# Front outputs of a gated two-branch attention kernel summed in one PSUM bank, with a new order of the main loop

## The chip, the core and the metric

The kernel runs on one core of a Trainium2 chip. Its engines are TensorE (PE, matrix products, with its weight loads listed as PEld), VectorE (DVE), ScalarE (ACT), GpSimd (POOL) and SyncE (SP, which issues most DMAs). Matmul results go to PSUM, which has eight banks of 512 fp32 numbers per partition; SBUF holds everything else. The metric is the device time of one execution in microseconds.

## The reference

One sequence of 2048 tokens with 512 features goes through two attention branches, and a gate mixes them.

```python
g = sigmoid((x * gate_w).sum(-1, keepdims=True))
# A: 32 heads of 16; each token sees 8 tokens, at distances 0, 2, ..., 14
q, k, v = split(x @ wqkv)
a = softmax(q . k[window] * 16**-0.5) @ v[window] @ wo_A
# B: 32 query heads of 16, one shared key and value head, all 2048 x 2048 pairs
q = x @ wq;  k = x @ wk;  v = x @ wv
b = softmax(q @ k.T * 16**-0.5) @ v @ wo_B
out = g * a + (1 - g) * b
```

All is fp32. The weights wq and wk of branch B are drawn eight times larger than the others, so the softmax of branch B needs the maximum of each row of scores before the exponential.

## The kernel before, in words

The program is unrolled, and the order of its instructions is written out by a planner that runs while the kernel is built: it keeps a clock for PE, ACT and DVE (`clk`), advances them by estimated durations (`T_R` for a matmul, `T_RED2` and `T_RED1` for the reductions of a pair and of a single, `T_TTR` for a sum of half scores, and so on), notes in `free` when each PSUM bank can be written again, and in `tasks` what is due later. Each engine then carries out its own list in that order and waits on semaphores where data or a buffer is not ready.

Branch B is cut into 32 units (a block of 512 queries, four heads) and each unit into 16 steps (128 keys), 512 steps in all. The work has three parts.

**Maxima.** For each unit, scores are computed once only to find row maxima: 64 half maxima of 128 queries x 512 keys each, 2048 in all. `fill_pair` computes two of them (heads on the even and on the odd 64 partitions, two matmuls side by side in the array) into the two-bank tile `pm` (`m2`), and DVE reduces both (L331). `fill_one` does one, into `ps` (`m1`) or, in the front, `po` (L342). In the front there is a cheaper form for two key blocks at a time: `fill_diff` computes half the difference (L390 into pm), ACT takes its absolute value (L399, `dd`), and `fill_sum` computes half the sum into ps and po, where DVE adds and takes the maximum in one instruction (L409). That form needs the half keys, which `half_keys` makes with the projections (L369). The maxima of a unit are collected in a small tile `mx`, which is first set to a very negative number by ACT (L305, the first nine). When a unit is complete, they are transposed, split and stored into two spare rows of its query tile `qst` (`shift_a` to `shift_d`).

**The front.** After a start of some 29 us, `stream` works through 14 query projections (`lumps` "q", 512 columns) and 64 projections for branch A, v and the gate ("a", 384 or 402 columns). Each output sums 12 products of 128 rows (x and the weights are split into two parts for precision). Each product is cut into its upper and lower 64 rows, which run side by side in the array as two lanes (`b` = 0, 1); the upper rows sum in the first and the lower in the second bank of an `eb` tile (pe), outputs alternate between the two tiles, and the very last uses pm. Both lanes advance by one product per turn of the loop. Maxima are put in between: a single takes the place of one lane's product, a pair or a diff goes between two. When an output is done, ACT copies both banks (`queries_post`: L201; `a_post`: L240 and L241, for v and the gate L243 and L244), and POOL adds the halves (L204, L250, L252, L253). The query is then split again (L210, L211) and stored; SP stores two finished A projections at a time from a `stage` tile, of which there are two. POOL meanwhile computes branch A itself (L518 to L578) from what was stored. At most eight units are stacked (`NB`) in the front, so that at most 512 half maxima can be made there.

**The main loop.** Each step has: the scores and exponential of the first two heads (`exp_pair(s, 0)`, L448 on PE and L450 on ACT, bank tile `e0`), one pair of maxima, the scores and exponential of the second two heads (`exp_pair(s, 1)`, `e1`), one single of maxima, and the weighted sums of the step before (`weighted`, L458, into po). The order is that of the tuple `order`; singles are left out where pairs alone suffice (`singles`) or where the bank is not free within `M1S` of the planner's clock. Three times four output rows are projected in a phase of their own (`out_phase`, through `stream`), with maxima in between; a phase starts when the maxima's lead falls below `LEAD` units or at a fixed step. The last four rows are spread over the last steps, when no maxima are left.

## Time and profile before

| | us |
|---|---|
| median of 3 runs | 1525.32 (1525.28 to 1527.5) |
| span of the profiled execution, first to last instruction | 1523.8 |
| PE busy | 1489.5 |
| ACT busy | 1243.8 |
| DVE busy | 1235.3 |
| POOL busy | 1030.6 |
| first and last projection matmul of the front start | 29.4 and 278.0 |
| first and last weighted sum of the main loop start | 279.5 and 1510.8 |

The profiled execution has its span of 1523.8 us and no time of its own beside it; the runs are 1.5 us longer in the median, which takes in what lies before the first and after the last instruction. The granted TensorE clock is 0.997 over the run.

How the rows read: in a group, "L399 ACT ACTIVATE dd<-pm ... x166 | 92.2, 610 | 21.8" means that line 399 wrote tile dd from tile pm on ACT 166 times, was busy for 92.2 us, took 610 ns each, and that ACT was idle for 21.8 us before them. In a stretch ("106.80:276.80") each engine's busy time is followed by its number of instructions; then come the granted clock, the DMA share and GB/s. In a timeline row the start and duration come first, merged instructions are counted (x2), and a bracket tells the idle time before and what ended it. In a wait row ("PEld pm L390 <- ACT dd L399: 13.6, 39, 1.6") the numbers are total us, times, and the longest. Matmul durations overlap: the spacing of starts is what PE needs.

### The profile page before, as it was taken

How to read it: one execution, taken by the hardware profiler on the slowest of the kernel's cores; microseconds unless marked ns; L12 is line 12 of the kernel's file. 1: busy time of each engine (PE TensorE's matmuls, PEld its weight loads, DVE VectorE, ACT ScalarE, POOL GpSimd, SP SyncE). 2: the span in 40 equal slices, each digit the busy share in tenths (PEclk: the TensorE clock that was granted, in tenths of full speed). 3: DMA queues.
4: the chain of work that ended last, by engine and by line, in shares of the span. 5: the costliest groups of instructions: out<-in, count | busy, mean ns of one | idle time of the engine just before them, and what ended most of it. 6: DMA issues, size and time to landing. Idle time of an engine off the chain costs nothing.

```text
span 1523.8 us, 28901 instructions
## 1 busy us (share of the span) xinstructions
PE 1489.5 (98%) x10920; PEld 706.1 (46%) x10920; DVE 1235.3 (81%) x1755; ACT 1243.8 (82%) x1590; POOL 1030.6 (68%) x1769
## 2 busy tenths in 40 slices
PE   7999999999999999999999999999999999999988
PEld 4989888533333333333333453333345335433333
DVE  5976666788888888889888998898899889888701
ACT  4558987889999899999999759999975995799774
POOL 7866988787888888888888888889887004100020
PEclk9999999999999999999999999999999999999999
DMA  6744223121121121120220112202201000000000
GB/s 216 202 119 131 90 75 126 33 75 47 50 76 47 41 75 44 43 76 22 66 77 14 65 33 68 68 12 69 69 19 33 1 1 16 15 2 2 1 1 28
DMA packets 43908, 85.63 MB, mean 56 GB/s; under 512 B 9520, under 2 KB 25960, under 8 KB 39672
## 3 DMA queue, kind: packets, MB, share of 16 engines
q1 hardware_dynamic: 36200, 44.00, 9.8%
q0 software_dynamic: 6560, 37.95, 7.5%
q8 instruction: 86, 1.41, 0.4%
q10 hardware_dynamic: 1008, 1.84, 0.3%
q14 instruction: 54, 0.44, 0.1%
HBM read 57.97 MB, written 25.25 MB: 55 GB/s over the span
## 4 chain that ended last, share of the span: by engine, by line
PE 89%; ACT 4%; DVE 4%; POOL 1%; issue 1%; DMA 1%; DVEq 0%; ACTq 0%; POOLq 0%
PE po L458 32%; PE pe L448 22%; PE pm L311 9%; PE ps L311 8%; PE pe L1004 8%; PE pe L709 4%; DVE mx L331 2%; ACT dd L399 2%; ACT pexp L450 1%; PE pm L766 1%; PE pm L390 1%; PE pe L174 1%; DVE mx L342 1%; PE po L390 0%; PE ps L390 0%
## 5 line engine op out<-in xcount | busy, mean ns | idle before, releaser
L450 ACT ACTIVATE pexp<-pe 128x1024 f32<-128x1024 f32 x1024 | 992.9, 1022 | 116.3 <-PE pe L448 116.0
L331 DVE TENSOR_REDUCE mx<-pm 128x2 f32<-128x1024 f32 x554 | 676.6, 1221 | 125.7 <-PE pm L311 120.4
L458 PE MATMUL po<-pexp,vst 128*32 128x512 f32 x4096 | 547.1, 606 | 0.6 <-DVE tt L472 0.5
L448 PE MATMUL pe<-qst,kst 64*128 64x512 f32 x2048 | 460.9, 448 | 6.8 <-ACT pexp L450 2.6
L448 PEld LDWEIGHTS pe<-qst,kst 64*128 64x128 f32 x2048 | 190.6, 184 | 506.7 <-ACT pexp L450 488.4
L342 DVE TENSOR_REDUCE mx<-ps 128x1 f32<-128x512 f32 x565 | 384.4, 680 | 5.7 <-PE ps L311 5.0
L311 PE MATMUL pm<-kst,qst 62*128 62x512 f32 x1122 | 235.7, 407 | 3.1 <-DVE mx L331 2.4
L311 PE MATMUL ps<-kst,qst 62*128 62x512 f32 x565 | 228.6, 405 | 0.7 <-DVE mx L342 0.7
L518 POOL TENSOR_TENSOR pr<-aext 128x256 f32<-128x256 f32 x256 | 182.0, 736 | 0.2
L578 POOL TENSOR_TENSOR oa<-oa,av 128x256 f32<-128x256 f32 x224 | 163.9, 732 | 15.4
L458 PEld LDWEIGHTS po<-pexp,vst 128*32 128x32 f32 x4096 | 80.7, 108 | 182.5 <-issue 170.7
L575 POOL TENSOR_TENSOR av<-aext,lg 128x256 f32<-128x256 f32 x224 | 139.3, 622 | 12.8
L484 POOL TENSOR_TENSOR rl<-rl,gate_t 128x16 f32<-128x16 f32 x31 | 6.8, 220 | 182.6 <-DVE rl L478 182.4
L311 PEld LDWEIGHTS pm<-kst,qst 62*128 62x128 f32 x1122 | 108.9, 186 | 24.7 <-DVE mx L331 21.3
L311 PEld LDWEIGHTS ps<-kst,qst 62*128 62x128 f32 x565 | 105.3, 186 | 22.4 <-DVE mx L342 18.4
L399 ACT ACTIVATE dd<-pm 128x512 f32<-128x512 f32 x166 | 92.2, 610 | 21.8 <-DVE mx L409 10.8
L1004 PE MATMUL pe<-wah,xh 64*128 64x384 f32 (+1 forms) x504 | 108.5, 338 | 0.0
L1004 PE MATMUL pe<-wal,xh 64*128 64x384 f32 (+1 forms) x504 | 108.5, 337 | 0.0
L1004 PE MATMUL pe<-wah,xl 64*128 64x384 f32 (+1 forms) x504 | 108.4, 337 | 0.0
L409 DVE CUSTOM_DVE_ANT_0 dd<-ps,dd 128x512 f32<-128x512 f32 x83 | 57.4, 692 | 58.8 <-PE ps L390 29.4
L524 POOL TENSOR_TENSOR tr<-pr 128x512 f32<-128x512 f32 x64 | 81.7, 1276 | 4.2
L250 POOL TENSOR_TENSOR stage<-stage,two 128x384 f32<-128x384 f32 x64 | 65.0, 1015 | 26.3 <-ACT two L241 13.4
(185 smaller groups left out, 1596.7 us busy)
## 6 DMA issues: line engine op xcount, KB each, us to landing
aext<-ad POOLq DMA_DIRECT2D x32, 1056.0 KB, 5.4
ad<-stage SPq DMA_DIRECT2D x32, 384.0 KB
qst<-qd SPq DMA_DIRECT2D x64, 128.0 KB
xraw<-xt SPq DMA_DIRECT2D x16, 256.0 KB
qd<-qhi SPq DMA_DIRECT2D x16, 256.0 KB
qd<-qlo SPq DMA_DIRECT2D x16, 256.0 KB
qst<-qd SPq DMA_DIRECT2D x64, 64.0 KB
qst<-ml SPq DMA_DIRECT2D x228, 2.0 KB
```

What stands on the lines that cost most here:

```text
L311: nc.tensor.matmul(dst, qst[v % NB][b:b + 62, pr, t * P:(t + 1) * P], kst[b:b + 62, kc * 512:(kc + 1) * 512], start=True, stop=True)
L331: nc.vector.tensor_reduce(m[:, :, pr, t, kc], dst, AX.X, ALU.max)
L342: nc.vector.tensor_reduce(m[:, odd, pr, t, kc:kc + 1], dst, AX.X, ALU.max)
L399: nc.scalar.activation(dd[0][:, odd], m2[:, odd, :], AF.Abs)
L448: nc.tensor.matmul(bank[:, odd, :], kst[b:b + 64, kt * P:(kt + 1) * P], qst[u % NB][b:b + 64, pr, :], start=True, stop=True)
L450: nc.scalar.activation(e, bank, AF.Exp, scale=SCALE)
L458: nc.tensor.matmul(po[32 * i:32 * i + 32, :], vst[:, kt, :], pexp[s, i // 2][:, i % 2, :], start=(kt == 0), stop=(kt == NJ - 1))
L518: nc.gpsimd.tensor_mul(pr[:, k], q, e[:, o:o + NH, AC:2 * AC])
L524: nc.gpsimd.tensor_add(nx, cur[:, :, 0:n], cur[:, :, n:2 * n])
L575: nc.gpsimd.tensor_mul(av, e[:, o:o + NH, 2 * AC:].rearrange("p j (h d) -> p j h d", d=DH), lg[:, w].unsqueeze(3).to_broadcast([P, NH, AG, ...
L578: nc.gpsimd.tensor_add(ao, ao, av)
L1004: nc.tensor.matmul(front[2 if x == last else x % 2][0][:, b, :n], l[h], r[h], start=(i == 0), stop=(i == 3 * C - 1))
```

## The change

1. In the front, both row halves of an output are summed in the same bank. Four single banks (`fb`, the halves of the two eb tiles) are used in turn, and the last two outputs use po and ps. The two lanes never write the same bank at once: the lower lane starts an output only when the upper lane has finished it and when a maximum (or an exponential) that was issued behind the upper lane's last product has been read, by the planner's clock (`marks`, `behind`); the first lower matmul is also given a dependency on that reading instruction. ACT copies an output once, and POOL's adds are gone. A query output is copied twice from PSUM, once as it is and once rounded, in place of the copy, the add and the split.
2. `front_stream` takes the place of `stream` in the front: it holds banks back for the half keys (`wanted`) instead of waiting for them, uses a lane only where the planner allows it (`below`, `after_upper`), and lets a diff wait until ACT's clock is at most `ACTS` ahead.
3. The first values of `mx` are set by ACT for two units alone and by POOL for the others, when the unit two before is complete.
4. In the main loop the single goes between the pair and the second scores: `(0, "m2", "m1", 1)` in place of `(0, "m2", 1, "m1")`.
5. Planner times: `T_R` 0.235, `T_TTR` 0.74, a projection product 0.1755 or 0.2335.

```diff
-LEAD, M2S, M1S = 1.5, 0.5, 0.3
-T_R, T_LAT, T_EXP, T_RED2, T_RED1, T_W, T_TTR = 0.23, 0.20, 0.92, 1.14, 0.61, 1.21, 0.66
+ACTS, LEAD, M2S, M1S = 0.5, 1.5, 0.5, 0.3
+T_R, T_LAT, T_EXP, T_RED2, T_RED1, T_W, T_TTR = 0.235, 0.20, 0.92, 1.14, 0.61, 1.21, 0.74
...
-    def queries_post(m, bank):
+    def queries_post(m, bank, key):
-        two = p0.tile([P, 2, 512], F32, name="two", tag="wqr", bufs=1)
-        nc.scalar.activation(two, bank, AF.Copy)
-        at = after("act", clk["pe"] + T_LAT, 0.92)
         own = p0.tile([P, 512], F32, name="qraw", bufs=1)
-        nc.gpsimd.tensor_add(own, two[:, 0], two[:, 1])
-        pool = max(pool, 1e3 * at) + 1400
         hi, lo = parts_of()
+        nc.scalar.activation(own, bank, AF.Copy)
+        nc.scalar.activation(hi, bank, AF.Copy)
+        at = after("act", clk["pe"] + T_LAT, 1.1)
+        free[key] = at + 0.1
...
-            nc.scalar.activation(hi, own, AF.Copy)
             nc.gpsimd.tensor_sub(lo, own, hi.bitcast(F32))
-            pool = max(pool, 1e3 * after("act", 0, 0.6)) + 1400
+            pool = max(pool, 1e3 * at) + 1400
...
-    def a_post(gg, j, x):
-        nonlocal pool
-        (bank, key), n = front[x], GN + (0 if gg else VN)
-        settle("add", 1)
+    def a_post(gg, j, bank, key):
         if j % 2 == 0:
             settle("store", 1)
             stage["t"] = p1.tile([P, GC, 2, AN], F32, name="stage", bufs=2)
         st = stage["t"]
-        if gg == 0 and j < 3:
-            two = wp.tile([P, GN + VN], F32, name="two", tag="aext", bufs=2)
-        else:
-            two = (p2 if j % 3 else pm)[0].tile([P, GN + VN], F32, name="two", tag=("two", "raw", "own")[j % 3], bufs=1)
-        own = st[:, :, j % 2, :]
-        nc.scalar.activation(own, bank[:, 0, :GN].rearrange("p (g n) -> p g n", g=GC), AF.Copy)
-        nc.scalar.activation(two[:, :n], bank[:, 1, :n], AF.Copy)
+        nc.scalar.activation(st[:, :, j % 2, :], bank[:, :GN].rearrange("p (g n) -> p g n", g=GC), AF.Copy)
         if gg == 0:
-            nc.scalar.activation(vst[:, j, 0:DH], bank[:, 0, GN:GN + DH], AF.Copy)
-            nc.scalar.activation(gate[:, 1, j:j + 1], bank[:, 0, GN + DH:GN + DH + 1], AF.Copy)
-        at = after("act", clk["pe"] + T_LAT, 0.8 if gg else 1.2)
+            nc.scalar.activation(vst[:, j, 0:DH], bank[:, GN:GN + DH], AF.Copy)
+            nc.scalar.activation(gate[:, 1, j:j + 1], bank[:, GN + DH:GN + DH + 1], AF.Copy)
+        at = after("act", clk["pe"] + T_LAT, 0.42 if gg else 0.8)
         free[key] = at + 0.1
-        def rest():
-            nonlocal pool
-            nc.gpsimd.tensor_add(own, own, two[:, :GN].rearrange("p (g n) -> p g n", g=GC))
-            if gg == 0:
-                nc.gpsimd.tensor_add(vst[:, j, 0:DH], vst[:, j, 0:DH], two[:, GN:GN + DH])
-                nc.gpsimd.tensor_add(gate[:, 1, j:j + 1], gate[:, 1, j:j + 1], two[:, GN + DH:GN + DH + 1])
-            pool = max(pool, 1e3 * at) + (1000 if gg else 1450)
-            if j % 2 == 1:
-                dst = ad[gg * GC:(gg + 1) * GC, HALO:, :].rearrange("g (p j) n -> p g (j n)", j=NJ)
-                tasks.append((pool / 1e3 + 0.5, lambda: nc.sync.dma_start(dst[:, :, (j - 1) * AN:(j + 1) * AN], st.rearrange("p g j n -> p g (j n)")), (), "store"))
-            if j == NJ - 1:
-                tasks.append((pool / 1e3 + 1.0, whole, (gg,)))
-        tasks.append((at, rest, (), "add"))
+        if j % 2 == 1:
+            dst = ad[gg * GC:(gg + 1) * GC, HALO:, :].rearrange("g (p j) n -> p g (j n)", j=NJ)
+            tasks.append((at + 0.3, lambda: nc.sync.dma_start(dst[:, :, (j - 1) * AN:(j + 1) * AN], st.rearrange("p g j n -> p g (j n)")), (), "store"))
+        if j == NJ - 1:
+            tasks.append((at + 1.0, whole, (gg,)))
...
+    marks, ups = [], [0]
+    def mark(inst, end):
+        marks.append((ups[0], end, inst.ins.name))
...
     def unit_tile(v):
         if v not in mx:
             mx[v] = wp.tile([P, 2, 2, 4, 4], F32, name="mx", bufs=3)
-            if v <= NB:
+            if v < 2:
                 nc.scalar.activation(mx[v].rearrange("p b i t k -> p (b i t k)"), ident[:, 0:64], AF.Identity, scale=0.0, bias=mk[:, 6:7])
+            elif v <= NB:
+                nc.gpsimd.memset(mx[v], -FMAX)
             left[v] = NF // NU
         return mx[v]
...
+            if v + 2 < NU:
+                unit_tile(v + 2)
...
+        got = nc.vector.tensor_reduce(m[:, :, pr, t, kc], dst, AX.X, ALU.max)
         free[key] = after("dve", after("pe", 0, T_R) + T_LAT, T_RED2) + 0.08
+        mark(got, free[key])
...
-    def half_keys(g):
-        keys = ("m2", "m2") if g == 0 else ("m1", "po")
+    wanted = []
+    def half_keys(g, keys):
         clk["pe"] = max(clk["pe"], *(free[k] for k in keys))
...
+            got = nc.scalar.activation(dd[0][:, odd], m2[:, odd, :], AF.Abs)
             ready_d[odd] = after("act", at, 0.52) + 0.1
+            mark(got, ready_d[odd])
...
+    fb = [eb[1][:, 0, :], eb[1][:, 1, :], eb[0][:, 0, :], eb[0][:, 1, :]]
+    def home(x):
+        if x >= last - 1:
+            return ((po, "po"), (m1, "m1"))[x - last + 1]
+        return fb[x % 4], f"f{x % 4}"
+    def begin(x):
+        lump = lumps[x]
+        if lump == ("a", 0, 3):
+            half_sel()
+        elif lump in (("a", 0, 4), ("a", 0, 6)):
+            wanted.append((1, ("m1", "po")) if lump[2] == 4 else (0, ("m2", "m2")))
+        items[x] = queries(lump[1]) if lump[0] == "q" else a_project(*lump[1:])
+    def begin_exp(k):
+        free[f"e{k}"] = max(free.get(f"f{y}", 0.0) for y in (2 - 2 * k, 3 - 2 * k))
+        exp_pair(0, k)
     def mm(b, at):
-        nonlocal pool
         x, i = at
         lump = lumps[x]
         if x not in items:
-            if lump[0] == "a" and lump[1:] == (0, 0):
-                settle("rest", 0)
-                p0.release()
-                branch_a()
-                pm.append(tc.alloc_tile_pool(name="maxima", bufs=1, side="right"))
-            if lump == ("a", 0, 3):
-                half_sel()
-            elif lump in (("a", 0, 4), ("a", 0, 6)):
-                half_keys(1 if lump[2] == 4 else 0)
-            items[x] = queries(lump[1]) if lump[0] == "q" else a_project(*lump[1:])
-            clk["pe"] = max(clk["pe"], free["m2" if x == last else f"e{x % 2}"])
+            begin(x)
         n = 512 if lump[0] == "q" else GN + (0 if lump[1] else VN)
         l, r = items[x][i]
         h = slice(64 * b, 64 * b + 64)
-        nc.tensor.matmul(front[2 if x == last else x % 2][0][:, b, :n], l[h], r[h], start=(i == 0), stop=(i == 3 * C - 1))
-        return T_R if n == 512 else 0.18
+        inst = nc.tensor.matmul(home(x)[0][:, :n], l[h], r[h], start=(i == 0 and b == 0), stop=(i == 3 * C - 1 and b == 1))
+        dur = 0.2335 if n == 512 else 0.1755
+        if b == 0 and x == last - 2 and i == 3 * C - 4:
+            ended.add(1)
+        if b == 0 and i == 3 * C - 1:
+            ups[0] = x + 1
+            if x == last:
+                begin_exp(1)
+        if b == 1 and i == 0:
+            tc.add_manual_dep(inst.ins, behind(x), mybir.DependencyInfo(mybir.DependencyClass.Sync, mybir.DependencyReason.DATA))
+        return dur
...
-        if x == last - 1 and i == 3 * C - 2:
-            ended.add(1)
-        if x == last and i in (2, 7):
-            exp_pair(0, int(i == 2))
+        if lump == ("a", 0, 0) and i == 1:
+            settle("rest", 0)
+            p0.release()
+            branch_a()
+            pm.append(tc.alloc_tile_pool(name="maxima", bufs=1, side="right"))
+        if x == last and i == 9:
+            begin_exp(0)
         if i < 3 * C - 1:
             return
+        items.pop(x)
+        bank, key = home(x)
         if lump[0] == "q":
             m = lump[1]
-            queries_post(m, eb[x % 2])
-            free[f"e{x % 2}"] = clk["act"]
+            queries_post(m, bank, key)
             ahead_wa(0, m - 4)
         else:
             gg, j = lump[1:]
-            a_post(gg, j, 2 if x == last else x % 2)
+            a_post(gg, j, bank, key)
             if gg + 1 < C:
                 ahead_wa(gg + 1, j - 2)
...
-    front = [(eb[0], "e0"), (eb[1], "e1"), (m2, "m2")]
-    stream([(x, i) for x in range(len(lumps)) for i in range(3 * C)], mm, done_mm, True)
+    def fits(key, slack=0.1):
+        return free[key] <= clk["pe"] + slack and not (wanted and key in wanted[0][1])
+    def front_stream(seq):
+        at, told = [0, 0], 0
+        may = (below, after_upper)
+        while told < len(seq):
+            if wanted and all(free[k] <= clk["pe"] + 0.1 for k in wanted[0][1]) and not pend:
+                half_keys(*wanted.pop(0))
+            single, odd = None, -1
+            if pend:
+                k = pend[0][4]
+                if free[("m1", "po")[k]] <= clk["pe"] + 0.1 and ready_d[k] <= clk["pe"] + 0.4:
+                    single, odd = fill_sum, k
+            elif ended or paired() and not half:
+                pass
+            elif half or slots and fillable():
+                for dst, key in ((m1, "m1"), (po, "po")):
+                    if single is None and fits(key):
+                        single, odd = lambda dst=dst, key=key: fill_one(dst, key), half[0][4] if half else 0
+            dur = 0.0
+            for b in (0, 1) if odd != 1 else (1, 0):
+                if b == odd:
+                    now = clk["pe"]
+                    single()
+                    clk["pe"] = now
+                elif at[b] < len(seq) and may[b](*seq[at[b]]):
+                    dur = max(dur, mm(b, seq[at[b]]))
+                    at[b] += 1
+            after("pe", 0, dur or T_R)
+            if ended:
+                if slots and fillable() and fits("m2"):
+                    fill_pair(m2, "m2")
+            elif paired():
+                if not half and not pend and not wanted and max(free["m2"], clk["dve"] - 1.2, clk["act"] - ACTS) <= clk["pe"] + 0.1:
+                    fill_diff()
+            elif slots and fillable() and fits("m2"):
+                fill_pair(m2, "m2")
+            while told < at[1]:
+                told += 1
+                done_mm(seq[told - 1])
+    def behind(x):
+        marks[:] = [m for m in marks if m[0] > x]
+        return next((m[2] for m in marks if m[1] + 0.1 <= clk["pe"]), None)
+    def after_upper(x, i):
+        return i > 0 or behind(x) is not None
+    def below(x, i):
+        return i > 0 or free.get(home(x)[1], 0.0) <= clk["pe"] + 0.1 and (lumps[x] != ("a", 0, 3) or bool(pm)) and not (pend and x >= last - 1)
+    front_stream([(x, i) for x in range(len(lumps)) for i in range(3 * C)])
...
-        order = (0, "m2", 1, "m1") if s > 1 else (1, "m2", 0, "m1") if s else ()
+        order = (0, "m2", "m1", 1) if s > 1 else (1, "m2", "m1", 0) if s else ()
```

36 lines of the change are left out of this document (12 added, 24 removed).

## The prediction

> **What bounds the kernel now.** I read the page first, then the busy time by stretches, then one step of the main loop in the timeline, then the waits.
>
> ```profile
> span 1523.8 us, 28901 instructions
> PE 1489.5 (98%) x10920; PEld 706.1 (46%) x10920; DVE 1235.3 (81%) x1755; ACT 1243.8 (82%) x1590; POOL 1030.6 (68%) x1769
> PE 89%; ACT 4%; DVE 4%; POOL 1%; issue 1%; DMA 1%; DVEq 0%; ACTq 0%; POOLq 0%
> ...
> 106.80:276.80 170.00, 166.47 (x1659) 149.88 (x1658) 112.79 (x349) 143.07 (x336) 135.23 (x220) 1.00 0.33 102
> 279.45:850.00 570.55, 567.15 (x3935) 203.36 (x3935) 502.72 (x629) 519.66 (x571) 484.39 (x909) 1.00 0.16 53
> 1309.00:1432.00 123.00, 122.99 (x862) 43.84 (x854) 108.64 (x130) 111.44 (x118) 8.82 (x20) 1.00 0.01 1
> 1441.00:1510.00 69.00, 62.71 (x357) 25.11 (x357) 2.16 (x5) 49.55 (x60) 12.64 (x16) 0.98 0.00 1
> ```
>
> The columns of a stretch are PE, PEld, DVE, ACT and POOL. TensorE is busy nearly throughout, and the chain is 89% PE. Two stages matter: the front's diff stage (106.8 to 276.8 us) and the main loop (279 to about 1441 us with maxima, then to 1510 without). In the main loop PE is full and ACT and DVE are both within some 10% of it, so I looked at which wait is closest behind PE. That takes one step:
>
> ```profile
> 599.55 1.94 ACT L450 ACTIVATE pexp<-pe 128x1024 f32<-128x1024 f32 x2 [0.19 <-PE pe L448]
> ...
> 601.08 0.19 PEld L448 LDWEIGHTS pe<-qst,kst 64*128 64x128 f32 x2 [0.84 <-ACT pexp L450]
> 601.09 0.49 PE L448 MATMUL pe<-qst,kst 64*128 64x512 f32 x2
> ...
> 601.42 0.40 PE L311 MATMUL pm<-kst,qst 62*128 62x512 f32 x2
> 601.54 0.19 PEld L448 LDWEIGHTS pe<-qst,kst 64*128 64x128 f32 x2 [0.16 <-ACT pexp L450]
> ...
> 601.66 0.39 PE L448 MATMUL pe<-qst,kst 64*128 64x512 f32 x2
> ...
> 601.86 1.23 DVE L331 TENSOR_REDUCE mx<-pm 128x2 f32<-128x1024 f32 x1 [0.32 <-PE pm L311]
> 601.89 0.40 PE L311 MATMUL ps<-kst,qst 62*128 62x512 f32 x1
> ...
> 603.00 0.68 DVE L342 TENSOR_REDUCE mx<-ps 128x1 f32<-128x512 f32 x1
> ...
> 603.55 0.40 PE L311 MATMUL pm<-kst,qst 62*128 62x512 f32 x2
> ```
>
> A step is 603.55 - 601.42 = 2.13 us. On PE the pair (pm) is followed 0.24 us later by the second scores (pe) and again 0.23 us later by the single (ps). The second scores' weight load comes 0.05 us after ACT ends (599.55 + 1.94 = 601.49, load at 601.54). The single had no wait: its bank is free at 603.00 + 0.68 = 603.68 and it is next wanted at 603.55 + 0.24 + 0.23 = 604.02. So in this order the ACT release only just suffices and the DVE release has about 0.3 us to spare.
>
> **The change part by part.**
>
> **Second evictions.**
>
> ```profile
> L399 ACT ACTIVATE dd<-pm 128x512 f32<-128x512 f32 x166 | 92.2, 610 | 21.8 <-DVE mx L409 10.8 <-PE pm L390 10.6
> L241 ACT ACTIVATE two<-pe 128x384 f32<-128x384 f32 (+1 forms) x63 | 31.5, 499 | 0.0
> L201 ACT ACTIVATE two<-pe 128x1024 f32<-128x1024 f32 x14 | 14.4, 1027 | 5.7 <-PE pe L1004 5.1
> L210 ACT ACTIVATE qhi<-qraw 128x512 fp32r<-128x512 f32 x14 | 8.9, 632 | 21.2 <-POOL qraw L204 14.1 <-DMA qd<-qhi 7.1
> L250 POOL TENSOR_TENSOR stage<-stage,two 128x384 f32<-128x384 f32 x64 | 65.0, 1015 | 26.3 <-ACT two L241 13.4
> PEld pm L390 <- ACT dd L399: 13.6, 39, 1.6
> PE ps L369 <- issue: 1.7, 1, 1.7
> ```
>
> ACT loses 31.5 us of copies for the projections. A query output keeps two copies out of PSUM at about 0.61 us (the L399 row has that form), 17.1 us in place of 14.4 + 8.9, so 6 us less. ACT in the front falls by some 37 us. PE does not get this as such, since ACT was not full (143.07 of 170). What PE can get back is at most the 13.6 us in which a diff's weight load waited for ACT; matmuls already under way cover about half, so I take -6 (0 to -10). POOL loses 65.0 us and the smaller adds of the queries, v and gate. POOL is almost idle late in the main loop (8.82 of 123), so that is worth 0. Each store of a projection no longer waits for POOL and is issued on SP's queue some 1 us earlier, ahead of the small transfers of the maxima that stood before it; 0 as well, hidden behind the two stage tiles, and where they ran out ACT would stand until a store has landed, with the Abs copies queued behind it. The wait of the half keys for two banks at once becomes a condition, which gives back the 1.7 us of the L369 row.
>
> **One bank, lower rows behind.** The trace of before has no held-back row half. Its cost is a delay that is paid once: the lower lane starts after the upper lane's 12 matmuls and after one maximum that was issued behind them has been read. The wait for that maximum is new; behind the waiting matmul everything on PE is queued, ACT and DVE with it.
>
> ```profile
> 179.73 0.50 PE L390 MATMUL pm<-kcd,qst 62*128 62x512 f32 x2
> 180.07 0.34 PE L1004 MATMUL pe<-wah,xh 64*128 64x384 f32 x2
> 180.24 0.34 PE L1004 MATMUL pe<-wal,xh 64*128 64x384 f32 x2
> ```
>
> Pairs of projection matmuls follow each other by 0.175 us, so 12 are 2.1 us; the maximum's way adds about 0.4 + 1.23 (the pm matmul until DVE starts, the reduction). I take +4; the ends are +2 (the early scores fill the idle lane at the end) and +8 (lag grows to a second output). Later lower halves find their maximum long read, 0 while the planner's order holds. The Trainium skill (PSUM — Partial Sum Buffer, section "PSUM bank collisions raise a hardware error") says that different row tiles cannot write one bank at the same time and that software has to keep them apart. No row of before shows it; were it not so here, the hold could be dropped, this term would be 0 and the sum 4 us lower.
>
> **More rounds of diffs.** A round (two diff matmuls, two sums, four half maxima) costs PE 0.34 + 0.235 = 0.575 us, from 179.73 to 180.07 and the single spacing in the step above.
>
> ```profile
> L409 DVE CUSTOM_DVE_ANT_0 dd<-ps,dd 128x512 f32<-128x512 f32 x83 | 57.4, 692 | 58.8 <-PE ps L390 29.4
> 106.80:276.80 170.00, 151.71 (x1328) 138.98 (x1327) 1.00 0.33 102
> ```
>
> Before, 83 rounds stand in 170 us, one in 2.05, among 1328/2 = 664 pairs (the second row is L1004 alone). Two Abs copies (2 x 0.61) and two sums on DVE (2 x 0.69 and a read-out each) allow one in about 1.8 once ACT has half the copies. I take 93 rounds: +10 x 0.575 = +6 us, and 40 half maxima more. The ends are 75 rounds (the new conditions on ACT and on wanted banks hold them back) and 100, since eight stacked units hold 512 half maxima and the front has 52 singles + 2 x 28 pairs + 4 x 83 = 440 now (the rows of L331 and of L342, the third of L342 in the main loop):
>
> ```profile
> 29.40:106.80 77.40, 34.25 (x28) 1.00 0.58 160
> 29.40:106.80 77.40, 33.47 (x52) 1.00 0.58 160
> 279.45:1441.00 1161.55, 375.95 (x553) 1.00 0.13 41
> ```
>
> The front: -6 - 1.7 + 4 + 6 = +2.3, range -10 to +12.
>
> **First values by GpSimd.** Most of the small ACT writes that set them go to POOL, and a unit's is issued two units early; 0, with POOL's idle 35 of 170 us as cover. Without that cover a round's sum on DVE would wait for POOL's queue, a few us a unit.
>
> **Single between pair and second scores.** PE's own work per step is the same. The single now wants its bank right after the pair: at 603.55 + 0.24 = 603.79. It is free at 603.68, its load can start 0.05 later, and a matmul behind a load that was waited for starts 0.10 later (0.49 against 0.39 in the rows at 601.09 and 601.66): 603.83 to 603.84. It is some 0.05 us late, and the second scores and the weighted sums queue behind it, since PE takes them in order. After a late step DVE gains that 0.05, so every other step is late: 0.025 us a step. DVE sets it, by 0.44 us from pair to reduction, 1.14 to the second one, and 0.68. The main loop has 553 singles, some 45 of them in its three output phases and a few in pauses; I take 485 steps with both: +12 us. Ends: 0, and +0.05 in each, +24. The Trainium skill (PSUM — Partial Sum Buffer, section "Engine vs sequencer instructions") says that matmuls start and complete in program order though a weight load may be pulled ahead. By that rule the late single delays all behind it and the sum is as here; by its opposite, scores that pass a waiting single, this term would be 0 and the time 1520. The step above shows the issued order, so the trace agrees as far as it goes.
>
> ACT's release of the second bank gets 0.24 us of slack. Eight copies of 0.63 us per run overrun ACT's 0.19 us idle in a step, which this hides: -2.
>
> ```profile
> L75 ACT ACTIVATE woh<-os 128x512 fp32r<-128x512 f32 x8 | 5.1, 632 | 0.0
> ```
>
> **Fewer singles.** Forty half maxima made in the front leave forty steps without a single. Such a step is bound by ACT's 1.94 us plus about 0.05 in place of 2.155: -6 (0 to -10). The new planner times change only the order, 0.
>
> **The sum.** 1523.8 + 2.3 + 12 - 2 - 6 = 1530.1 us of span. The runs shown have a median of 1525.3, 1.5 over this span, which I take for what lies around it: 1532.
>
> **The rivals.**
> The single's wait does not bind (faster). If DVE reads the pair 0.05 us earlier, or the planner's skipped singles give DVE air often enough, the term of 12 is 0 and the rest is 1523.8 + 2.3 - 2 - 6 + 1.5 = 1520; with the front's low end 1507. For it: the overrun is only 0.05 us, the size of one semaphore. Against: DVE's chain is the same to 0.01 us in each step I looked at. It decides at a time from pair to free bank of 2.21 us, against 603.68 - 601.42 = 2.26.
>
> The held-back lower half starves the front (slower). Late marks or blocked banks leave half of PE empty again and again: 64 projections x 0.25 to 0.35 us = 16 to 22 us instead of 4, which gives 1544 to 1550. For it: a mark needs a maximum, and in the queries' stage DVE is full. Against: four banks, and a lag once built stays.
>
> The copies taken from ACT do nothing (no gain in the front): the front is PE's 664 x 0.175 = 116 and 83 x 0.575 = 48, so 164 of 170 us are matmuls already, and the 6 us do not come: 1538. This lies within the forecast's own range.
>
> **How the numbers follow.** Forecast 0.50 with its own range 1525 to 1541, first rival 0.32, second 0.18. A measurement of this kernel can tell about 0.2%, 3 us, from no change. Faster takes most of the first rival and a little of the forecast, 0.32; same 0.10; slower 0.58. 1510 to 1549 leaves out the far end of the first and of the second.
>
> **What would show it.** Of the main loop: steps of 2.13 and 2.18 us in turn, the load of ps waiting about 0.05 us for L342, the 0.16 us waits of pe gone. Of the front: it ends near 281 us with about 93 rounds, no copy of a second half, the first lower half some 4 us behind. Wrong would be: main steps still at 2.13 us, or a front that ends more than 10 us earlier or later.

## The result and the profile after

The changed kernel takes 1629.01 us (median of 4 runs, 1624.84 to 1631.02), the kernel before beside it 1526.34 us. The ratio is 1.0666, 95% interval 1.0648 to 1.0683: some 102 us slower, far outside the forecast's range.

The page of the changed kernel:

```profile
span 1623.0 us, 28701 instructions
PE 1523.4 (94%) x10920; PEld 713.2 (44%) x10920; DVE 1233.0 (76%) x1736; ACT 1219.8 (75%) x1531; POOL 948.6 (58%) x1670
PE 81%; ACT 7%; DVE 4%; issue 1%; DMA 0%; POOL 0%; SPq 0%; DVEq 0%; ACTq 0%
```

TensorE was busy for 98% of the span and is now for 94%, and the chain of work that ended last has 7% ACT in place of 4%. Where that lies is told by the stretches (columns PE, PEld, DVE, ACT, POOL, clock). The first fence is the front before. The second is of after: the whole front, its part with diffs, and the first 478 us of the main loop.

```profile
29.60:278.00 248.40, 241.51 (x2320) 217.46 (x2318) 182.41 (x442) 183.42 (x411) 197.09 (x290) 1.00 0.41 120
```

```profile
32.00:371.10 339.10, 272.68 (x2359) 231.54 (x2360) 202.61 (x476) 159.22 (x354) 152.75 (x263) 0.99 0.31 94
106.80:371.10 264.30, 205.69 (x1847) 178.66 (x1847) 140.81 (x394) 140.25 (x315) 122.42 (x232) 0.99 0.25 80
372.40:850.00 477.60, 471.63 (x3248) 165.84 (x3247) 398.20 (x490) 431.68 (x472) 403.00 (x757) 0.99 0.17 54
```

The front grew from 248.4 to 339.1 us, with only 39 matmuls more. TensorE stands for 66 of those 339 us, and no other engine is full: ACT and POOL do less than before. From the first to the last weight load of the weighted sums the main loop went from 1230.8 (279.5 to 1510.3) to 1237.4 us (372.4 to 1609.8). So 90.7 of the 99.2 us of span are the front's. What TensorE waited for there, in total us, times, and the longest (PE rows and PEld rows tell of the same time and are not added):

```profile
PE pe L992 <- ACT stage L230: 44.4, 44, 1.9
PE pe L992 <- ACT gate L233: 13.7, 15, 1.8
PE pe L992 <- ACT qhi L203: 7.6, 11, 1.3
PE pe L992 <- DVE kst L179: 1.9, 1, 1.9
PEld pe L992 <- ACT stage L230: 57.9, 43, 2.3
ACT dd L390 <- PE pm L381: 101.5, 87, 2.6
```

Projection products wait 70 times for ACT's copies of finished outputs, 65.7 us; before, the projections wait once for such a copy, 0.4 us. And ACT waits 101.5 us for the diffs, which stand in TensorE's queue behind the waiting products: the two engines hold each other up in turn. In the groups this reads as follows (L992 is the front's projection, L401 the sum of a round; x89 rounds in place of 83):

```profile
L390 ACT ACTIVATE dd<-pm 128x512 f32<-128x512 f32 x178 | 97.1, 596 | 103.7 <-PE pm L381 101.5
L992 PE MATMUL pe<-wah,xh 64*128 64x384 f32 (+1 forms) x496 | 142.9, 354 | 31.2 <-ACT stage L230 21.3
L401 DVE CUSTOM_DVE_ANT_0 dd<-ps,dd 128x512 f32<-128x512 f32 x89 | 61.6, 692 | 87.4 <-PE ps L381 73.9
```

One such place in the timeline:

```profile
249.24 1.09 ACT L390 ACTIVATE dd<-pm 128x512 f32<-128x512 f32 x2 [0.36 <-PE pm L381]
250.22 0.49 ACT L230 ACTIVATE stage<-pe 128x384 f32<-128x384 f32 x1
250.76 0.18 PEld L992 LDWEIGHTS pe<-wah,xl 64*128 64x128 f32 x1 [1.76 <-ACT stage L230]
250.76 0.44 PE L992 MATMUL pe<-wah,xl 64*128 64x384 f32 x1 [1.38 <-ACT stage L230]
252.16 0.40 PE L381 MATMUL pm<-kcd,qst 62*128 62x512 f32 x2
252.60 1.10 ACT L390 ACTIVATE dd<-pm 128x512 f32<-128x512 f32 x2 [1.89 <-PE pm L381]
```

ACT copies an output at 250.22, behind two Abs copies. TensorE stands for 1.38 us and goes on at 250.76, 0.05 us after the copy's end (250.71). The diff behind it comes at 252.16, and ACT has stood for 1.89 us when it gets it. The rows name the tile, pe, and not the bank: that the bank waited for is another one than the bank written is what the first and the second of the experiments below show.

In the main loop the forecast's pattern is there, steps of 2.19 and 2.13 us in turn, and the load of ps waiting for DVE (0.22 and 0.17 us, where the forecast had about 0.05):

```profile
600.24 0.40 PE L297 MATMUL pm<-kst,qst 62*128 62x512 f32 x2
600.42 0.18 PEld L297 LDWEIGHTS ps<-kst,qst 62*128 62x128 f32 x1 [0.22 <-DVE mx L331]
602.43 0.40 PE L297 MATMUL pm<-kst,qst 62*128 62x512 f32 x2
602.55 0.18 PEld L297 LDWEIGHTS ps<-kst,qst 62*128 62x128 f32 x1 [0.17 <-DVE mx L331]
604.56 0.40 PE L297 MATMUL pm<-kst,qst 62*128 62x512 f32 x2
```

The waits of the main loop have these loads 389 times in the changed kernel (first fence) and 61 times, of another kind and up to 0.8 us, before (second fence):

```profile
PEld ps L297 <- DVE mx L331: 82.6, 389, 0.4
```

```profile
PEld ps L311 <- DVE mx L342: 17.7, 61, 0.8
```

### The profile page after: what moved, and what is told of

The parts are those of the page before. It is cut to its first block, busy times and chain, and to the rows that moved or that the text cites. A ratio compares the mean times of both kernels' runs of the same rounds, so it can differ in the third digit from the quotient of the medians.

```text
span 1623.0 us, 28701 instructions
## 1 busy us (share of the span) xinstructions
PE 1523.4 (94%) x10920; PEld 713.2 (44%) x10920; DVE 1233.0 (76%) x1736; ACT 1219.8 (75%) x1531; POOL 948.6 (58%) x1670
## 3 DMA queue, kind: packets, MB, share of 16 engines
q10 hardware_dynamic: 1008, 1.84, 0.3%
## 4 chain that ended last, share of the span: by engine, by line
PE 81%; ACT 7%; DVE 4%; issue 1%; DMA 0%; POOL 0%; SPq 0%; DVEq 0%; ACTq 0%
PE po L452 30%; PE pe L441 23%; PE pm L297 8%; PE pe L992 7%; PE ps L297 4%; PE pe L690 4%; ACT dd L390 3%; DVE mx L319 2%; ACT pexp L443 2%; ACT stage L230 1%; PE pm L381 1%; PE pm L747 1%; PE po L381 1%; DVE mx L331 1%; PE ps L381 1%
## 5 line engine op out<-in xcount | busy, mean ns | idle before, releaser
L319 DVE TENSOR_REDUCE mx<-pm 128x2 f32<-128x1024 f32 x570 | 695.9, 1221 | 166.1 <-PE pm L297 156.3
L441 PE MATMUL pe<-qst,kst 64*128 64x512 f32 x2048 | 571.2, 456 | 6.6 <-ACT pexp L443 2.9
L441 PEld LDWEIGHTS pe<-qst,kst 64*128 64x128 f32 x2048 | 234.4, 185 | 445.7 <-ACT pexp L443 430.8
L331 DVE TENSOR_REDUCE mx<-ps 128x1 f32<-128x512 f32 x516 | 350.4, 679 | 0.0
L390 ACT ACTIVATE dd<-pm 128x512 f32<-128x512 f32 x178 | 97.1, 596 | 103.7 <-PE pm L381 101.5
L992 PE MATMUL pe<-wah,xh 64*128 64x384 f32 (+1 forms) x496 | 142.9, 354 | 31.2 <-ACT stage L230 21.3
L992 PE MATMUL pe<-wah,xl 64*128 64x384 f32 (+1 forms) x496 | 141.1, 345 | 19.1 <-ACT stage L230 16.9
L992 PE MATMUL pe<-wal,xh 64*128 64x384 f32 (+1 forms) x496 | 137.6, 343 | 9.0 <-ACT stage L230 6.2
L297 PEld LDWEIGHTS ps<-kst,qst 62*128 62x128 f32 x516 | 95.1, 184 | 87.0 <-DVE mx L331 82.6
L401 DVE CUSTOM_DVE_ANT_0 dd<-ps,dd 128x512 f32<-128x512 f32 x89 | 61.6, 692 | 87.4 <-PE ps L381 73.9
L992 PEld LDWEIGHTS pe<-wah,xh 64*128 64x128 f32 x496 | 83.0, 187 | 44.5 <-ACT stage L230 29.1
L992 PEld LDWEIGHTS pe<-wah,xl 64*128 64x128 f32 x496 | 85.2, 187 | 25.4 <-ACT stage L230 21.3
```

The costliest lines, as they stand in the source:

```text
L297: nc.tensor.matmul(dst, qst[v % NB][b:b + 62, pr, t * P:(t + 1) * P], kst[b:b + 62, kc * 512:(kc + 1) * 512], start=True, stop=True)
L319: got = nc.vector.tensor_reduce(m[:, :, pr, t, kc], dst, AX.X, ALU.max)
L331: got = nc.vector.tensor_reduce(m[:, odd, pr, t, kc:kc + 1], dst, AX.X, ALU.max)
L390: got = nc.scalar.activation(dd[0][:, odd], m2[:, odd, :], AF.Abs)
L441: nc.tensor.matmul(bank[:, odd, :], kst[b:b + 64, kt * P:(kt + 1) * P], qst[u % NB][b:b + 64, pr, :], start=True, stop=True)
L992: inst = nc.tensor.matmul(home(x)[0][:, :n], l[h], r[h], start=(i == 0 and b == 0), stop=(i == 3 * C - 1 and b == 1))
```

## The experiments

My theory after the comparison: the four banks of the changed front are the halves of two tiles of two banks each, and a product that writes one half is made to wait for the copy that reads the other half. Rivals: the wait for a maximum (the forecast's second rival), and copies that are late by themselves. Chips differ a little between the groups of runs, so ratios to the kernel before on the same chip are compared.

### Own banks

```diff
+    pf = [... pool "front0" on the left, "front1" on the right ...]
-    fb = [eb[1][:, 0, :], eb[1][:, 1, :], eb[0][:, 0, :], eb[0][:, 1, :]]
+    fb = [pf[k].tile([P, 512], F32, name=f"pe{k}{h}") for k in (1, 0) for h in range(2)]
...  # begin_exp(k): pf[k] is released, and the two-bank tile eb[k] of the main loop allocated in its place
```

> The changed kernel with the four front banks as four tiles of one bank each (in the changed kernel two banks are one tile); the two-bank tiles of the scores are made when the front ends. Theory (a matmul into one bank waits for the copy out of its neighbour, since both are one tile): the waits of projection matmuls for ACT's copies nearly go, the front's last projection starts at 280 to 295 us instead of 368, and the time is 1540 to 1560 us. Rival (holding the lower half back and the lag itself starve the front): the front still ends beyond 340 us and the time stays above 1600 us.

1538.25 us (1536.27 to 1540.91), a little below the 1540 to 1560 I had expected, ratio 1.0072 (1.0055 to 1.0089). Against 1.0666 that is 0.0594, 90.7 us. (The profiled spans differ by 84.2 us only. In the front of own_banks the clock was at half for 13.7 us, in that of the changed kernel for 3.4 us; the last experiment is on this.) The front runs from 31.4 to 286.5 us in place of 32.0 to 371.1, with the same 2359 matmuls, the same 89 rounds and the same 478 half maxima made by its end. Of TensorE's waits in the front there is left:

```profile
PE pe L995 <- DVE kst L181: 1.8, 1, 1.8
PE pm L299 <- DVE mx L321: 1.1, 1, 1.1
PE pm L383 <- ACT dd L392: 0.8, 3, 0.3
PE ps L383 <- DVE mx L403: 0.4, 1, 0.4
```

None of the 70 waits is there. The hold on the lower lane, its wait for a maximum, the marks and the copies are all unchanged. So the loss is the sharing of a tile, and nothing else of the new front.

### One tile shared

The dose: outputs 2, 3, 6, 7, ... share a tile again.

```diff
-    fb = [pf[k].tile([P, 512], F32, name=f"pe{k}{h}") for k in (1, 0) for h in range(2)]
+    fb = [pf[1].tile([P, 512], F32, name=f"pe1{h}") for h in range(2)]
+    shared = pf[0].tile([P, 2, 512], F32, name="pe0")
+    fb += [shared[:, 0, :], shared[:, 1, :]]
```

> Own banks, with one of the two tiles whole again: outputs 0, 1, 4, 5, ... of the front have tiles of one bank each, outputs 2, 3, 6, 7, ... share one tile of two banks, as all do in the changed kernel. Theory (a product waits for the copy of the neighbouring bank of its tile): half of the 91 us that own tiles took away come back, the front ends some 45 us later than with own banks, 325 to 340 us, total 1575 to 1595. Rival (the time lies in something that moving to four tiles changed by accident, such as where the banks lie): the time stays near 1538 or goes back to 1629.

1582.06 us, ratio 1.0347 (1.0331 to 1.0363): 0.0275 above own banks, 42 us, of 0.0594 with both. The front ends at 326.0. The waits are half of those with both tiles shared:

```profile
PE pe L997 <- ACT stage L234: 20.9, 23, 1.4
PE pe L997 <- ACT gate L237: 6.5, 7, 1.8
PE pe L997 <- ACT qhi L207: 3.9, 5, 1.2
```

Half the sharing gives half the waits and half the time. The theory holds.

### The place of the single

The order of the step, `(0, "m2", "m1", 1)` against `(0, "m2", 1, "m1")`, was put back in the changed kernel and in own banks, and put alone into the kernel before.

```diff
-        order = (0, "m2", "m1", 1) if s > 1 else (1, "m2", "m1", 0) if s else ()
+        order = (0, "m2", 1, "m1") if s > 1 else (1, "m2", 0, "m1") if s else ()
```

> The changed kernel with the old order of the main loop (single after the second scores). Theory of the late single, as predicted: steps go from alternately 2.13 and 2.18 us back to 2.13 us, and the time falls by 8 to 14 us, to about 1618 us. Rival (the late single is absorbed elsewhere): within 3 us of the changed kernel, 1629 us.

> Front banks as tiles of their own and the old order of the main loop: what is left of the change is the front's single copies and POOL's first values. Theory: 10 to 14 us below own_banks, 1528 to 1548 us, so that the two causes add. If the front's gain of some 6 us from ACT is real it shows as a front that ends by 285 us with over 440 half maxima made.

> The kernel before with nothing but the new order of the main loop. Theory of the late single: +8 to +14 us, 1534 to 1541 us, and about half of the steps at 2.18 us. Rival: 1526 us, no change, because where a step is late the next one is not.

| kernel | order | time, us | ratio (95%) | steps with a pair and a single: mean us (count) | singles in the main loop |
|---|---|---|---|---|---|
| after | new | 1629.01 | 1.0666 (1.0648 to 1.0683) | 2.163 (366) | 492 |
| after_old_order | old | 1615.15 | 1.0578 (1.0558 to 1.0598) | 2.137 (378) | 524 |
| own_banks | new | 1538.25 | 1.0072 (1.0055 to 1.0089) | 2.162 (368) | 492 |
| own_banks_old_order | old | 1528.51 | 1.0000 (0.9987 to 1.0013) | 2.137 (382) | 524 |
| before_new_order | new | 1550.64 | 1.0161 (1.0146 to 1.0176) | 2.160 (365) | 509 |
| before | old | 1527.15 | 1 | 2.134 (400) | 554 |

The step lengths are worked out from the traces: from the first weighted sum of a step to that of the next, for steps under 2.6 us with one reduction of a pair and one of a single. In each of the three pairs of kernels the new order makes such a step 0.024 to 0.027 us longer, which is what the forecast had.

That is not where the loss shows, though. From the first weighted sum of the loop to that of its step 487, own_banks takes 1155.0 us and own_banks_old_order 1153.1; the changed kernel takes 1156.8 and after_old_order 1153.2. So other steps have become shorter and give most of it back. The planner leaves out 32 to 45 singles, since by its clock the bank is not free at the new place, and those maxima must be made elsewhere. Step 487 takes 9.27 us in own_banks and 2.10 in own_banks_old_order: the loop has run out of maxima and makes four pairs of them in the banks of the scores, at VectorE's pace:

```profile
1445.69 0.50 PE L299 MATMUL pe<-kst,qst 62*128 62x512 f32 x2 [0.92 <-DVE mx L321]
1446.82 0.50 PE L299 MATMUL pm<-kst,qst 62*128 62x512 f32 x2 [0.63 <-DVE mx L321]
```

In the kernel before with the new order there are three such steps, of 9.3, 15.1 and 12.7 us, where before has one of 5.7. From 1360 us to the same late step the work then takes 118 us (first row, before_new_order) in place of 94 (second row, before):

```profile
1360.00:1478.00 118.00, 101.92 (x609) 36.02 (x606) 89.71 (x100) 76.56 (x84) 11.05 (x22) 0.87 0.01 1
1360.00:1454.00 94.00, 90.69 (x606) 31.84 (x606) 70.95 (x84) 80.94 (x87) 8.79 (x17) 0.96 0.01 1
```

These 24 us are as much as the whole loss of 23.5 us, which is twice the 8 to 14 I had expected. TensorE stands for 16 us there in place of 3, and the granted clock is 0.87 in place of 0.96. In the changed kernel, whose front makes 38 half maxima more, the order costs 0.0072 to 0.0088, 11 to 13 us. By the medians own_banks_old_order is 9.7 us below own_banks, just under the 10 to 14 expected; by ratios it is 11. Its front made 478 half maxima (over 440 expected), but ended at 286.8 us rather than by 285.

So the changed kernel with own banks and the old order takes as long as the kernel before. That was less than I had hoped for, and the next experiments ask what eats the front's gain.

### First values by GpSimd, alone

```diff
-            if v <= NB:
+            if v < 2:
                 nc.scalar.activation(mx[v]..., scale=0.0, bias=mk[:, 6:7])
+            elif v <= NB:
+                nc.gpsimd.memset(mx[v], -FMAX)
...
+            if v + 2 < NU:
+                unit_tile(v + 2)
```

> The kernel before with one part of the change alone: the first values of the maxima of units 2 to 8 written by GpSimd two units ahead, in place of small ACT writes. Theory: 0, within 3 us of before, since GpSimd has the time. Rival (a unit's values come late, because GpSimd's queue is in order and long in the front): 5 to 15 us slower, with waits of a sum or a reduction on GpSimd in the front.

1523.15 us against 1527.84, ratio 0.9970 (0.9958 to 0.9981): 4.6 us faster, where I had 0. A row of before that is gone is that of DVE's sums waiting for the small ACT write. The second fence is the tile's rows in this kernel, where GpSimd writes them:

```profile
DVE dd L409 <- ACT mx L305: 5.4, 5, 2.0
```

```profile
L307 POOL MEMSET mx<- x6: 150/152/173, 85.9 to 246.7; 128x64 f32 x6
L305 ACT ACTIVATE mx<-ident,mk x1: 337/337/337, 40.4 to 40.4; 128x64 f32<-128x64 f32 x1
```

A write of 0.34 us stood behind ACT's queue of Abs copies, and DVE stood behind it, five times and up to 2.0 us. But DVE's sums now wait 27.0 us for the Abs copies themselves, in place of 21.1, so that this row explains the gain is not shown. The front ends 2.0 us earlier (276.0). In the main loop, 1229.4 in place of 1230.8 us, the difference is within what runs differ by.

### The front's start and the stacked queries

Two further losses stood in the trace of own_banks_old_order. At 30 us TensorE stands for 1.84 us, since the first product goes into the bank of the last keys, and then the granted clock is at half:

```profile
31.75 0.57 PE L995 MATMUL pe<-xh,wqh 64*128 64x512 f32 x1 [1.83 <-DVE kst L181]
331.61 1.02 PE L299 MATMUL pm<-kst,qst 62*128 62x512 f32 x2 [3.65 <-DMA qst<-qd]
```

```profile
32.00:44.00 12.00, 12.00 (x41) 9.28 (x41) 8.50 (x11) 0.90 (x3) 4.62 (x4) 0.50 0.14 42
```

The second fence is the stretch from 32 to 44 us, with the clock (0.50) as its third number from the end. The other loss is the second row of the first fence: a pair that waits 3.65 us for the queries of unit 8, which the planner believes landed.

```diff
-        pk = fb[2 - 2 * (t % 2)]
+        pk = fb[2 + t % 2]
```

```diff
-        stacked.append(clk["pe"] + 5.0)
+        stacked.append(clk["pe"] + (5.0 if u < NB else 9.0))
```

> Own banks with the old place of the single, and the four key products of the start put into the third and fourth bank of the front, so that the first product of the front's stream no longer waits for VectorE to have read the last keys (a pause of 1.84 us of TensorE at 30 to 32 us in own_banks and in its run with the old order, after which the granted clock was 0.50 up to 44 us). Theory (the pause is what lets the clock fall): the pause goes, the front's first 13 us run at full clock, 6 to 9 us less than the 1528.5 of the run with the old order: 1519 to 1523. Rival (the clock falls there for another reason): only the pause goes, about 2 us, 1526 to 1527, the clock still 0.50.

> As keys_apart, and the planner allows 9.0 in place of 5.0 us until the stacked queries of units 8 and later have landed. In the run with own banks and the old order a maximum waited 3.65 us for them at 328 us, with all of TensorE's queue behind it. Theory: that wait goes, the steps meanwhile run without a pair at ACT's pace: 2 to 4 us less than keys_apart. Rival (the missing pairs are then made in pauses of the loop): 0.

keys_apart: 1529.58 us, ratio 1.0010 (1.0001 to 1.0019), no gain; I had expected 1519 to 1523. The pause is gone and the front's first product starts at 28.0 us, but two things follow. The maximum behind it now meets a split on VectorE that takes 5.34 us, while GpSimd works through seven splits; TensorE then stands for 4.31 us. And the clock falls at 31.8 us, before that pause:

```profile
31.55 0.46 PE L995 MATMUL pe<-xh,wql 64*128 64x512 f32 x1
31.80 0.63 PE L995 MATMUL pe<-xh,wqh 64*128 64x512 f32 x1
37.60 0.80 PE L299 MATMUL pm<-kst,qst 62*128 62x512 f32 x2 [4.31 <-DVE mx L321]
```

```profile
31.07 5.34 DVE L78 TENSOR_TENSOR wql<-wqr,wqh 128x512 fp32r<-128x512 f32 x1
```

So the clock can fall without the pause that I had blamed. keys_apart_stack: 1523.97 us, ratio 0.9970 (0.9959 to 0.9981), 5.6 us less than keys_apart; I had 2 to 4. The wait for the stacked queries (3.4 us in keys_apart) is gone from its trace. So is a stretch of 3.4 us at half clock that followed the wait in keys_apart, from 332.1 to 335.5, which I had not counted. The first 24 steps of the loop take 50.8 in place of 56.2 us, and that is nearly all of the 5.6.

### What lets the clock fall

In all these fronts the upper rows work alone at first, since the lower lane is held back. fill_pause puts four full-height products into the pause, both_halves lets the lower rows run along with the upper rows' first output, fill_both does both.

```diff
+    for c in range(C):                      # fill_pause, fill_both: behind the three first maxima
+        nc.tensor.matmul(fb[3], wkr[:, c, :], xraw[3, c], start=(c == 0), stop=(c == C - 1))
...
+        if b == 0 and x == 0:               # both_halves, fill_both: beside each upper product of the first output
+            nc.tensor.matmul(fb[3], l[64:128], r[64:128], start=(i == 0), stop=(i == 3 * C - 1))
```

> Own banks, old place of the single, the longer allowance for stacked queries (as keys_apart_stack, but with the keys in their old banks), and four products more: the last key's products once again into a bank that nobody reads, placed behind the three first maxima, where TensorE stands 1.84 us for VectorE. It adds work that is thrown away. In five runs with this front the granted clock was 0.5 from about 32 to 44 us, which costs some 6 us. Theory (the pause lets the clock fall): the clock stays at 1.00, 1517 to 1520. Rival (it falls for another reason, as it did at 31.8 us in keys_apart before that run's pause): 1523 to 1526, clock 0.5 up to 44 us.

> As fill_pause without the four products, but with twelve others: while the upper rows work on the front's first output alone, the lower rows repeat each product on their own rows into a bank that nobody reads yet (thrown away). Beside the upper rows' they take no time. Theory (the clock falls because half of the array stands still): the clock stays at 1.00, 1517 to 1520. Rival: 1523 to 1526, clock 0.5 up to 44 us.

> fill_pause and both_halves together. If either of the two is the reason for the fall of the clock, or only both together, it stays at 1.00 here: 1517 to 1521. If neither is, 1523 to 1527.

fill_pause 1519.88 us, ratio 0.9955 (0.9941 to 0.9969); both_halves 1520.15, 0.9956 (0.9941 to 0.9972); fill_both 1521.14, 0.9960 (0.9948 to 0.9973). The stretch from 32 to 44 us in fill_pause and in both_halves, and the pause that both_halves keeps:

```profile
32.00:44.00 12.00, 12.00 (x78) 9.46 (x78) 11.33 (x14) 1.57 (x4) 4.62 (x5) 1.00 0.15 47
```

```profile
32.00:44.00 12.00, 11.80 (x94) 10.01 (x92) 12.00 (x15) 1.41 (x4) 5.39 (x4) 1.00 0.15 42
```

```profile
31.18 0.50 PE L995 MATMUL pe<-xh,wqh 64*128 64x512 f32 x1 [1.84 <-DVE kst L181]
```

Both edits keep the clock at 1.00 here, and the times are as the theory of each had them, within 0.2 us. One trace is weak evidence, though. The changed kernel and after_old_order have the same front, with the same pause, and the clock stayed in the one (first row) and fell at 33.2 us in the other (second row):

```profile
32.00:44.00 12.00, 11.31 (x70) 8.69 (x72) 11.80 (x15) 2.20 (x5) 5.85 (x5) 1.00 0.16 46
32.00:44.00 12.00, 12.00 (x50) 9.42 (x48) 9.37 (x11) 0.55 (x2) 4.29 (x4) 0.57 0.16 49
```

The number of matmuls is no evidence either, since fewer fit in at half clock. All runs together say more: none of the thirteen runs of fill_pause, both_halves and fill_both has a mean clock below 0.997. Of the ten runs of own_banks_old_order, three have 0.997 (1522.62, 1522.79 and 1524.92 us) and seven 0.991 to 0.994 (1527.33 to 1530.98; the profiled one is of these). Twelve us at half clock are 6 us, which is 0.004 of the run, so I take the three for runs in which the clock did not fall. The fall costs about 6 us and does not come in every run.

Neither the pause nor the idle lower rows is the reason by itself. both_halves keeps the pause; in fill_pause no lower projection product runs from 33.1 to 38.3 us, at clock 1.00; in keys_apart the clock falls with no pause over 0.3 us. That a little more work between 28 and 36 us is enough, wherever it is put, is what the thirteen runs show; why, they do not. One rival was not tried, the place of the pause in the clock's own rhythm. In the clock records of every trace the stretches of one clock, up to the last, are whole multiples of 3.413 us. In own_banks_old_order the whole pause lies in the 3.41 us before the fall, in after_old_order all but 0.3 us of it. In both_halves (29.3 to 31.2 us) and in the changed kernel (30.1 to 32.0) such a limit, at 30.3 and 31.4 us, divides it.

Against keys_apart_stack the gain is 0.0014 to 0.0015, about 2 us by runs whose intervals overlap, though the front ends 4 to 5.5 us earlier (281.9 and 280.5 against 286.0). That kernel differs in the place of the keys too; one with the longer allowance alone was not run.

fill_pause beats both kernels: 0.45% below the kernel before, and some 108 us below the changed one (0.9955 against 1.0666). It is the changed front with tiles of one bank, the old place of the single, the longer allowance, and four products that nobody reads.

## Why the prediction was wrong

**The step that failed** is "One bank, lower rows behind", and in it the sentence "Later lower halves find their maximum long read, 0 while the planner's order holds". That wait was indeed about 0: among TensorE's waits in the changed front, no projection product waits for a maximum (the first waits 1.9 us for the last keys). But it was the only wait I priced. I took the four banks for independent because the planner keeps a free time for each. The waits that the program carries are kept per tile, and two outputs now lived in one tile, one being written while the other is copied. In the kernel before an output had a whole tile of two banks to itself and one release, so its trace could not show it; the diff could (`fb` lists halves of `eb`). The term was +4, with +8 as its far end; the sharing alone cost 91 us. The front ended at 371.1 us, where the forecast had named more than 10 us away from 281 as a sign of being wrong. The lag was 6.4 us in the changed kernel (first upper product at 31.96, first lower at 38.35) for the forecast's some 4; what it costs by itself was not tried.

The Trainium skill (PSUM — Partial Sum Buffer, section "The four PSUM rules") says that each bank is a separate physical memory. The runs agree: with own tiles, products go on while the neighbouring bank is copied, and the 70 waits are gone. The wait was the program's and not the chip's.

**The second rival** had the place right (half of TensorE left empty again and again in the front) and named late marks or blocked banks, at 0.25 to 0.35 us for each of 64 projections. It is a copy and not a mark that is late, the bank is blocked by its neighbour, and the loss is 91 us over 78 outputs, 1.2 us each, since every wait also delays the diff behind it, and with it ACT's next copy.

**Second evictions and half keys, -7.7.** Right as far as it can be seen; no run has this part alone. In the front of own_banks ACT is busy for 157.6 us in place of 183.4, and the loads of diffs wait 3.4 us for ACT in place of 13.6; the half keys' row of 1.7 us is gone. The stretch and the wait in own_banks:

```profile
31.40:286.50 255.10, 252.83 (x2359) 234.74 (x2360) 197.79 (x476) 157.55 (x354) 149.81 (x258) 0.97 0.41 124
```

```profile
PEld pm L383 <- ACT dd L392: 3.4, 10, 0.6
```

**More rounds.** 89 for the forecast 93, and 478 half maxima for 480, since singles and pairs of the ordinary form made 14 more than before (478 - 4 x 89 = 122, against 440 - 4 x 83 = 108).

**The front's sum, +2.3, ending near 281 us.** With the tiles apart and the clock whole (both_halves) it ends at 280.5, with own tiles and the clock at half at 286.5. So without the shared tile and the fall of the clock the end is where the forecast had it. Some of that is luck: the sum held neither the pause of 1.84 us at the start nor the 2.0 us that the first values give.

**First values by GpSimd, 0.** Mis-sized: -4.6 us alone. I looked at what GpSimd would be asked to do, and not at who waited for ACT's small writes; the row with 5.4 us stood in the trace. That it is the cause is not shown.

**Single between pair and second scores, +12 and -2.** The step was right: 0.026 us longer for the forecast 0.025, and 389 loads wait. The sum was not. Up to step 487 the order costs 1.9 us in own banks and 3.6 us in the changed kernel, much as the first rival had it (skipped singles give DVE air), though which steps give the time back was not followed. Most of the rest is in the late step of 9.3 us in which the left-out maxima are made up; that price I had put at nothing. That the whole came to 11 to 13 us is luck: in the kernel before it came to 23.5. The -2 was not tried by itself.

**Fewer singles, -6.** The main loop with the old order is 5.0 us shorter than before in after_old_order (1225.8) and 2.1 in own_banks_old_order (1228.7). The term is of the right size, with 30 singles fewer for the forecast 40, but something that I had not seen eats part of it: with its lead of maxima the loop comes to unit 8 before that unit's queries have landed, and a pair waits 3.0 to 4.2 us for them in each of these fronts, with TensorE's queue behind it. The kernel before has no such wait.

Put together, from before to after by ratios: shared tiles 0.0594 (91 us), the place of the single 0.0072 (11 us), and all the rest 0.0000. In that rest the gains of the front, of the first values and of the fewer singles stand against the clock (about 6 us) and the stacked queries (5.6 us).

## What to carry to other kernels

Before two streams of work are put into one buffer, look at what the waits are kept for: if it is the tile, two banks of one tile are one buffer, and a planner that keeps them apart plans a schedule that the program does not carry out. A moved bank is therefore priced by who else touches its tile. In an in-order queue a wait returns with interest (65.7 us of waits here, 91 us of time), because what feeds the releasing engine stands behind it. And a longer step times the number of steps is no price where the planner answers by leaving work out: follow that work to where it is done.

## What the runs showed of the hardware

The granted clock fell to 0.50 in a stretch in which TensorE's rows show it busy all the time: 12.00 of 12 us in own_banks_old_order from 32 to 44, with 41 matmuls, each on 64 or 62 of the 128 rows. It came back at 45.7 us, after products of both halves had run side by side since 41.1 us. Upper projection products without lower ones, some maxima beside them, did not bring it back in these 9 us at half clock, and did not make it fall in fill_pause in 5 us at full clock. In all thirteen traces the clock is 0.50 or 1.00, and each stretch of one of them, up to the last, lasts a whole multiple of 3.413 us. The Trainium skill (TensorE: Matmul & The Clock Gate, section "What's actually happening") knows two states, half and full clock, and says that about 3.4 us of sustained activity bring the full one. The two states agree with these traces, 0.50 and 1.00; that a busy TensorE leaves the half state after one such window does not, since it stayed there for 12 us with no pause. What amount of work decides, and why the fall does not come in every run, stays open.

The split of 128x512 numbers on VectorE took 5.34 us in keys_apart, where the same form took 0.68 us at 25.4 us in the same trace, while GpSimd ran seven splits in a row from 27.13 to 35.85 us. Why was not tried.
